# Moving one of four small weight-folding steps from inside a projection stage to the border before the output stage, with a new order of the output parts

## Chip, cores, metric

One core of a Trainium2 chip (trn2). The metric is device time in microseconds (us) of one execution, inputs and outputs in HBM. Lower is better.

## The reference, cut to what matters

Two attention blocks on the same 2048 x 1024 input, mixed by a gate. Block A is linear attention with 32 heads of 32, block B a dilated local attention:

```python
x = A_x
g = _sigmoid((x * gate_w).sum(-1, keepdims=True))
a = _A_ref(x, A_wqkv, A_wo)      # ... num = einsum("bhqd,bhde->bhqe", pq, kv); o = num / den; o @ wo
b = _B_ref(x, B_wqkv, B_wo)      # ... 8 keys per query, two apart; o @ wo
return g * a + (1 - g) * b
```

In block A each head's `kv` is only 32 x 32. The kernel multiplies it into that head's 32 rows of `A_wo` once, which gives a matrix "W2", so that the output is `pq` (normalized) times W2 and no `num` is ever made.

## The kernel before

TensorE works through: A's keys, a Gram matrix, `kv`; a stage with B's values and A's queries (here "value stage"); a B stage, in which B's keys and queries are projected as 64x64 matmuls with the attention in between; and an output stage, 128x128 matmuls that add A's and B's output products in one bank. W2 is made in four "events". Each folds one quarter of it (`g` chooses four of the eight row blocks, `half` the columns): 16 matmuls of 32x32 with 512 columns, one on each 32x32 part of the array, into four PSUM banks, and four copies that write the result over the old weights.

```python
def w2_event(g, half, engines=(nc.vector.tensor_copy, nc.scalar.copy)):
    def go():
        w2p = [ps_1.tile([P, 512], F32, name="w2_ps", tag="p1") for _ in range(4)]
        for j in range(4):
            for r in range(4):
                rs = slice(32 * r, 32 * r + 32)
                nc.tensor.matmul(w2p[r][32 * j:32 * j + 32, :],
                                 lhsT=KVT[rs, 4 * g + j, (r % 2) * 32:(r % 2) * 32 + 32],
                                 rhs=WoA[half][rs, 4 * g + j, :], start=True, stop=True)
        for r in range(4):
            engines[r % len(engines)](out=WoA[half][:, 4 * g + r, :], in_=w2p[r][:])
    return go

units = [u for t in range(4) for u in v_units(t)]        # one 128x128 matmul each
w2_event(0, 0)()
interleave(units, [(20, w2_event(0, 1)), (40, w2_event(1, 0))])
# ... twelve times: 16 value matmuls, 16 query matmuls
w2_event(1, 1, (nc.scalar.copy,))()
# ... B stage, then the output stage:
parts = [(tb, c0, n) for tb in range(NB)                 # row block, first column, columns
         for c0, n in ([(0, 512), (512, 512)] if tb < NB - 1 else [(0, 512), (512, 256), (768, 128), (896, 128)])]
first = [out_part(i, *p_) for i, p_ in enumerate(parts[:7])]
for k in range(2):          # A's half of seven parts, then B's half of them
    for f in first:
        f(k)
# ... then one part after the other; odd parts take banks of ps_3, even ones of ps_pj
```

So the first event lies between the `kv` matmuls (128x64) and the value stage, the second and third lie inside the value stage, the fourth lies between it and the B stage.

The softmax here doesn't subtract the row's maximum and nothing guards it: scores larger than these inputs give would overflow.

Of the kernel before, what the change touches and what calls it, by code (L numbers as in the profile page):

```python
# [11 lines left out]
F32 = mybir.dt.float32  # L12
# [3 lines left out]
P = 128  # L16
# [11 lines left out]
def interleave(units, events):  # L28

    events = sorted(events, key=lambda e: e[0])  # L30
    for i, unit in enumerate(units):
        while events and events[0][0] <= i:
            events.pop(0)[1]()
        unit()
    for _, fn in events:
        fn()
# [3 lines left out]
def kernel(  # L40
# [11 lines left out]
    nc = tc.nc  # L52
# [12 lines left out]
    NB = S // P  # L65
# [10 lines left out]
    def load_w(name, src, col0, tag, only=(0, 1)):  # L76
        halves = []
        for h in only:
            w = wpool.tile([P, KT, 512], BF16, name=f"{name}{h}", tag=tag)
            c0 = col0 + h * 512  # L80
            nc.sync.dma_start(out=w[:], in_=src[:, c0:c0 + 512].rearrange("(kt p) n -> p kt n", p=P))
            halves.append(w)
        return halves
# [19 lines left out]
    with tc.manual_schedule(engines={SP, mybir.EngineType.Activation}):  # L103
# [17 lines left out]
        WoA = load_w("WoA", A_wo, 0, "wo")  # L121
# [18 lines left out]
    for slot in range(2):  # L140
        nc.gpsimd.memset(qsel[:, slot:slot + 1], 0.0)
        for pair in range(2):
            r = 64 * pair + 32 * slot
# [5 lines left out]
    KVT = consts.tile([P, KT, 64], BF16, name="KVT")  # L149
# [3 lines left out]
    def phi(work, dst, pj):  # L153
# [2 lines left out]
        nc.vector.tensor_scalar(out=e[:], in0=e[:], scalar1=1.0, scalar2=1e-6, op0=ALU.min, op1=ALU.add)  # L156
        nc.vector.scalar_tensor_tensor(out=dst, in0=pj[:], scalar=0.0, in1=e[:], op0=ALU.max, op1=ALU.add)

    with tc.manual_schedule(engines={PE}):

        with ExitStack() as s1:
            ps_1 = s1.enter_context(tc.tile_pool(name="ps_1", bufs=4, space=bass.MemoryType.PSUM))
# [41 lines left out]
            for t in range(1, NB):  # L204
                side.append(lambda t=t: nc.vector.tensor_tensor(
                    out=zacc[:], in0=zacc[:] if t > 1 else pk[:, 0, :], in1=pk[:, t, :], op=ALU.add))
            side.append(lambda: nc.gpsimd.partition_all_reduce(zrow[:], zacc[:], P, bass_isa.ReduceOp.add))
            for t in range(NB):
                side.append(lambda t=t: nc.vector.tensor_tensor_reduce(
                    out=gjunk[:], in0=xrow[:, t, :], in1=gw_row[:], scale=1.0, scalar=0.0, op0=ALU.mult,  # L210
# [3 lines left out]
            for half in range(2):  # L214
                g_ = junk.tile([P, KT, 512], BF16, name=f"G{half}", tag=f"G{half}")
                G.append(g_)
                for kt in range(KT):
                    pj = ps_pj.tile([P, 512], F32, name="g_ps", tag="pj")
                    for t in range(NB):
                        nc.tensor.matmul(pj[:], lhsT=xrow[:, t, kt * P:(kt + 1) * P],  # L220
                                         rhs=pk[:, t, half * 512:(half + 1) * 512],
                                         start=(t == 0), stop=(t == NB - 1))
# [11 lines left out]
            for g in range(2):  # L234
                kvp = ps_pj.tile([P, 512], F32, name="kv_ps", tag="pj")[:, 0:256].rearrange("p (c d) -> p c d", c=4)
                for c in range(4):
                    for kt in range(KT):
                        for j in range(2):
                            cols = slice(c * P + 64 * j, c * P + 64 * j + 64)
                            nc.tensor.matmul(kvp[64 * j:64 * j + 64, c, :], lhsT=WvA[g][:, kt, cols],  # L240
                                             rhs=G[g][:, kt, cols], start=(kt == 0), stop=(kt == KT - 1))
# [32 lines left out]



            def w2_event(g, half, engines=(nc.vector.tensor_copy, nc.scalar.copy)):
                def go():
                    w2p = [ps_1.tile([P, 512], F32, name="w2_ps", tag="p1") for _ in range(4)]
                    for j in range(4):  # L280
                        for r in range(4):
                            rs = slice(32 * r, 32 * r + 32)
                            nc.tensor.matmul(w2p[r][32 * j:32 * j + 32, :],  # L283
                                             lhsT=KVT[rs, 4 * g + j, (r % 2) * 32:(r % 2) * 32 + 32],
                                             rhs=WoA[half][rs, 4 * g + j, :], start=True, stop=True)
                    for r in range(4):
                        engines[r % len(engines)](out=WoA[half][:, 4 * g + r, :], in_=w2p[r][:])
                return go

            def v_units(t):  # L290
                def mm(half, kt, st):
                    if kt == 0:
                        st["pj"] = bank1()
                    nc.tensor.matmul(st["pj"][:], lhsT=xT[:, kt, t * P:(t + 1) * P], rhs=WvB[half][:, kt, :],  # L294
                                     start=(kt == 0), stop=(kt == KT - 1))
                    if kt < KT - 1:
                        return
                    v = Vst[t % 2]
                    nc.scalar.copy(out=v[:, half * 16:(half + 1) * 16, 0:Dh],  # L299
                                   in_=st["pj"][:].rearrange("p (h e) -> p h e", h=16))  # L300
                    if half == 1:
                        nc.sync.dma_start(out=vd[t * P:(t + 1) * P, :], in_=v.rearrange("p h e -> p (h e)"))
                        if t % 8 == 7:
                            load_v(t // 8)
                for half in range(2):
                    st = {}
                    for kt in range(KT):
                        yield lambda half=half, kt=kt, st=st: mm(half, kt, st)
# [35 lines left out]
                    nc.sync.dma_start(out=pqd[t * P:(t + 1) * P, :], in_=pn)  # L344

            units = [u for t in range(4) for u in v_units(t)]
            w2_event(0, 0)()
            interleave(units, [(20, w2_event(0, 1)), (40, w2_event(1, 0))])
            for t in range(12):
                for u in v_units(4 + t):  # L350
                    u()
                for u in qa_units(t, bank1, qa_finish):
                    u()
            w2_event(1, 1, (nc.scalar.copy,))()
            WqB = load_w("WqB", B_wqkv, 0, "wc")


# [4 lines left out]
        with ExitStack() as s2:  # L362
# [164 lines left out]
            for c in range(KT):  # L527
                kts[c] = kpool.tile([P, 2, 1024], BF16, name="kt", tag="kt")
                for hh in range(2):
# [3 lines left out]
                    if 1 <= c <= 2:  # L533
                        t = 2 * (c - 1) + hh
                        nc.sync.dma_start_transpose(out=pqT[0][:, :, t * P:(t + 1) * P],
                                                    in_=pqd[t * P:(t + 1) * P, :])
                    if 4 <= c < 7:
# [6 lines left out]
                              in_=B_wo[4 * P:, 512:1024].rearrange("(k p) n -> p k n", p=P))  # L544
# [20 lines left out]
        with ExitStack() as s3:  # L565
            work3 = s3.enter_context(tc.tile_pool(name="work3", bufs=3))
            ps_3 = s3.enter_context(tc.tile_pool(name="ps_3", bufs=4, space=bass.MemoryType.PSUM))
            pqT.append(big.tile([P, KT, 1536], BF16, name="pqT1", tag="vV"))
            for r0 in (512, 1024):
                nc.sync.dma_start_transpose(out=pqT[1][:, :, r0 - 512:r0], in_=pqd[r0:r0 + 512, :])  # L570

            def qa_late(t):
                r = raw[:, t - 12, :]
                for half in range(2):
                    h = slice(half * 512, (half + 1) * 512)
                    phi(work3, r[:, h], r[:, h])
                pn = lw[:, t - 12, :]
                normalize(t, r, pn, fw[:, t % 2, :])
                nc.sync.dma_start_transpose(out=pqT[1][:, :, (t - 4) * P:(t - 3) * P], in_=pn)

            def out_part(i, tb, c0, n):

                st = {}

                def mm(side, c):
                    if side == 0 and c == 0:
                        st["ps"] = ps_3.tile([P, 512], F32, name="e3_ps", tag="p3") if i % 2 else \
                            ps_pj.tile([P, 512], F32, name="d3_ps", tag="pj")
                    if side == 0:
                        lhsT, W = (pqT[0][:, c, tb * P:(tb + 1) * P] if tb < 4 else  # L590
                                   pqT[1][:, c, (tb - 4) * P:(tb - 3) * P]), WoA
                    else:
                        lhsT, W = OBT[:, c, tb * P:(tb + 1) * P], WoB
                    nc.tensor.matmul(st["ps"][:, 0:n], lhsT=lhsT, rhs=W[c0 // 512][:, c, c0 % 512:c0 % 512 + n],  # L594
                                     start=(side == 0 and c == 0), stop=(side == 1 and c == KT - 1))
                    if side == 0 or c < KT - 1:
                        return
                    osb = work3.tile([P, 512], BF16, name="osb", tag="e")
                    dst = rows(out2, tb * P, (tb + 1) * P)[:, c0:c0 + n]
                    if i == len(parts) - 1:  # L600
                        nc.vector.tensor_scalar(out=osb[:, 0:n], in0=st["ps"][:, 0:n], scalar1=omg[:, tb:tb + 1],  # L601
                                                scalar2=None, op0=ALU.mult)
                        nc.sync.dma_start(out=dst, in_=osb[:, 0:n])
                        return
                    nc.scalar.activation(out=osb[:, 0:n], in_=st["ps"][:, 0:n], func=ACT.Copy,
                                         scale=omg[:, tb:tb + 1])
                    nc.scalar.dma_start(out=dst, in_=osb[:, 0:n])

                def side(k):
                    for c in range(KT):  # L610
                        mm(k, c)
                return side

            parts = [(tb, c0, n) for tb in range(NB)
                     for c0, n in ([(0, 512), (512, 512)] if tb < NB - 1 else [(0, 512), (512, 256), (768, 128), (896, 128)])]
            first = [out_part(i, *p_) for i, p_ in enumerate(parts[:7])]
            for k in range(2):
                for f in first:
                    f(k)
            for i, p_ in enumerate(parts):  # L620
                if i < 7:
                    continue
                if i % 2 == 1 and i < 15:
                    qa_late(12 + (i - 7) // 2)
                f = out_part(i, *p_)
                f(0)
                f(1)
# [31 lines left out]
```

## Time and profile before

| | before |
|---|---|
| time, median of three runs | 472.55 us (472.46 to 472.68) |
| span of the profiled run | 471.2 us |
| TensorE busy | 467.1 us |
| value stage, from its first weight load to the B stage's | 98.11 us |
| B stage, from its first weight load to the output stage's | 140.65 us |
| output stage, from its first weight load to the start of the last VectorE instruction | 110.86 us |

From the page of before, busy time of each engine, and the chain that ended last:

```profile
PE 467.1 (99%) x5765; PEld 270.9 (57%) x5765; DVE 276.6 (59%) x600; ACT 168.0 (36%) x274; POOL 15.4 (3%) x30
...
PE 98%; DMA 1%; DVE 0%; issue 0%; DVEq 0%
```

The view of waits of before, for TensorE (who waited for what: us in total, times, longest):

```profile
PE warm L175 <- PEq L643: 0.8, 1, 0.8
PE pk_ps L169 <- DMA xT<-in_A_x_dram: 0.5, 1, 0.5
```

TensorE never waits for another engine after its start. Whatever the change does, it must do it to TensorE's own stream, or by a new wait of TensorE.

The chain of before in order of time (start, length, what), around the first three events. `w_ps` is an event, `p_ps` are value matmuls:

```profile
116.50 2.15 PE kv_ps L240 x128
118.64 0.36 PE w_ps L283 x16
119.01 4.42 PE p_ps L294 x20
123.43 0.36 PE w_ps L283 x16
123.80 4.42 PE p_ps L294 x20
128.22 0.36 PE w_ps L283 x16
```

Read the distance from one row's start to another's, not the lengths: 119.01 to 123.80 is 4.79 us for twenty matmuls and one event, while twenty matmuls alone take 20 x 0.2158 = 4.32 us.

The timeline of before at the edge of B stage and output stage, weight loads only (start, length, line, shape, count, idle time before and what ended it):

```profile
356.23 1.06 PEld L389 LDWEIGHTS <-xT 64*64 64x64 bf16 x20
357.69 0.11 PEld L594 LDWEIGHTS <-pqT 128*128 128x128 bf16 x2 [0.41 <-issue]
```

No event is here, and yet the weight loads pause 0.41 us, for nothing that the profile can name: the array changes from 64x64 to 128x128. The matmuls lose less than this pause. Within a form each weight load starts 0.21 us, one slot, ahead of its matmul; the first one after a change starts together with it (0.004 us ahead here), so only about 0.1 us of the pause is lost time, as measured below.

### The profile page before, as it was taken

Reading aid. Unit: us, or ns where it says so; the run is one execution under the profiler, and the core shown is the slowest. Engines: PE = TensorE matmul, PEld = TensorE weight load, DVE = VectorE, ACT = ScalarE, POOL = GpSimd, SP = SyncE. Lnnn points to the kernel's source line nnn. Section 1 sums busy time; section 2 is a strip of 40 time slices with the busy share of each in tenths; the row PEclk is TensorE's granted clock in tenths of the full one; section 3 lists DMA queues with packets and bytes.
Section 4 is the critical chain, followed back from the end, with each engine's and each line's share of the span. In section 5 each row is a group of like instructions: output and inputs, shape, how many; then the busy total and the mean of one; then the engine's idle time right before and its main releaser. Section 6 shows DMA issues by size and latency. Waiting matters only on the chain.

```text
span 471.2 us, 13192 instructions
## 1 busy us (share of the span) xinstructions
PE 467.1 (99%) x5765; PEld 270.9 (57%) x5765; DVE 276.6 (59%) x600; ACT 168.0 (36%) x274; POOL 15.4 (3%) x30
## 2 busy tenths in 40 slices
PE   8999999999999999999999999999999999999997
PEld 5444444445444444444888888888875444444444
DVE  0596689990319999999667676767660049800000
ACT  1343321102433333334555555555551134221121
POOL 3300000500000000000000000000000000000000
PEclk9999999999999999999999999999999999999999
DMA  8999970000643233527326526432563913221001
GB/s 206 208 234 379 349 255 0 0 1 0 217 137 112 85 142 126 155 97 246 106 57 103 115 50 93 101 87 57 94 168 71 230 61 79 70 54 45 34 33 46
DMA packets 98732, 55.40 MB, mean 118 GB/s; under 512 B 70130, under 2 KB 90610, under 8 KB 98674
## 3 DMA queue, kind: packets, MB, share of 16 engines
q1 hardware_dynamic: 93378, 49.87, 41.1%
q10 hardware_dynamic: 5296, 4.69, 3.0%
q8 instruction: 45, 0.74, 0.7%
q14 instruction: 13, 0.11, 0.1%
HBM read 26.10 MB, written 15.86 MB: 89 GB/s over the span
## 4 chain that ended last, share of the span: by engine, by line
PE 98%; DMA 1%; DVE 0%; issue 0%; DVEq 0%
PE q_ps L389 26%; PE d_ps L594 12%; PE pk_ps L169 12%; PE p_ps L294 12%; PE g_ps L220 12%; PE e_ps L594 12%; PE p_ps L330 9%; PE po L469 2%; PE s2b L447 2%; DMA xT<-in_A_x_dram 1%; PE kv_ps L240 0%; PE w_ps L283 0%; DVE osb L601 0%; DVEq L601 0%
## 5 line engine op out<-in xcount | busy, mean ns | idle before, releaser
L389 PE MATMUL q_ps<-xT,WqB 64*64 64x512 bf16 x1024 | 70.3, 376 | 0.0
L389 PE MATMUL q_ps<-xT,WkB 64*64 64x512 bf16 x1024 | 69.8, 376 | 0.0
L156 DVE TENSOR_SCALAR e<-e 128x512 f32<-128x512 f32 x64 | 27.1, 423 | 66.3 <-ACT e L155 66.3
L294 PE MATMUL p_ps<-WvB,xT 128*128 128x512 bf16 x256 | 57.6, 379 | 0.0
L169 PE MATMUL pk_ps<-WkA,xT 128*128 128x512 bf16 x256 | 55.8, 381 | 0.5 <-DMA xT<-in_A_x_dram 0.5
L220 PE MATMUL g_ps<-pk,xrow 128*128 128x512 bf16 x256 | 55.4, 379 | 0.0
L452 ACT ACTIVATE PT<-s2b 128x928 bf16<-128x928 f32 (+4 forms) x40 | 34.2, 856 | 50.0 <-PE s2b L447 49.0
L454 DVE TENSOR_TENSOR PT<-PT,mask 128x928 bf16<-128x928 bf16 (+4 forms) x40 | 23.6, 590 | 35.6 <-ACT PT L452 35.5
L389 PEld LDWEIGHTS <-WkB 64*64 64x64 bf16 x1024 | 40.3, 107 | 7.0 <-DMA vd<-tmp 0.2
L330 PE MATMUL p_ps<-WqA,xT 128*128 128x512 bf16 x192 | 43.4, 379 | 0.0
L594 PEld LDWEIGHTS <-pqT 128*128 128x128 bf16 x272 | 26.0, 98 | 29.8 <-issue 0.4
L594 PEld LDWEIGHTS <-OBT 128*128 128x128 bf16 x272 | 26.0, 98 | 29.3
L169 PEld LDWEIGHTS <-xT 128*128 128x128 bf16 x256 | 25.0, 98 | 31.0 <-DMA xT<-in_A_x_dram 0.8
L389 PEld LDWEIGHTS <-WqB 64*64 64x64 bf16 x1024 | 39.4, 107 | 5.6 <-DVE qz L429 0.2
L220 PEld LDWEIGHTS <-xrow 128*128 128x128 bf16 x256 | 25.0, 98 | 30.2
L294 PEld LDWEIGHTS <-xT 128*128 128x128 bf16 x256 | 24.8, 98 | 30.2 <-issue 0.7
L601 DVE TENSOR_SCALAR osb<-e_ps,omg 128x128 bf16<-128x128 f32 x1 | 0.4, 351 | 57.6 <-PE e_ps L594 57.6
L155 ACT ACTIVATE e<-pk_ps 128x512 f32<-128x512 f32 x32 | 18.9, 597 | 40.7 <-PE pk_ps L169 36.5
L469 PEld LDWEIGHTS <-PT 64*56 64x56 bf16 (+2 forms) x1152 | 30.1, 104 | 4.4
L330 PEld LDWEIGHTS <-xT 128*128 128x128 bf16 x192 | 18.8, 98 | 22.7
L299 ACT CAST tmp<-p_ps 128x512 bf16<-128x512 f32 x32 | 18.8, 589 | 36.1 <-PE p_ps L294 32.5
L594 PE MATMUL d_ps<-WoA,pqT 128*128 128x512 bf16 (+1 forms) x136 | 30.9, 370 | 0.0
(63 smaller groups left out, 543.5 us busy)
## 6 DMA issues: line engine op xcount, KB each, us to landing
vd<-tmp SPq DMA_DIRECT2D x16, 264.0 KB
xrow<-in_A_x_dram SPq DMA_DIRECT2D x4, 1024.0 KB
out_dram<-osb ACTq DMA_DIRECT2D x31, 128.0 KB
pqd<-tmp SPq DMA_DIRECT2D x12, 256.0 KB
WvA<-in_A_wqkv_dram SPq DMA_DIRECT2D x2, 1024.0 KB
WoA<-in_A_wo_dram SPq DMA_DIRECT2D x2, 1024.0 KB
WvB<-in_B_wqkv_dram SPq DMA_DIRECT2D x2, 1024.0 KB
WqA<-in_A_wqkv_dram SPq DMA_DIRECT2D x2, 1024.0 KB
```

Source lines behind the costliest of these rows:

```text
L155: nc.scalar.activation(out=e[:], in_=pj[:], func=ACT.Exp)
L156: nc.vector.tensor_scalar(out=e[:], in0=e[:], scalar1=1.0, scalar2=1e-6, op0=ALU.min, op1=ALU.add)
L169: nc.tensor.matmul(pj[:], lhsT=xT[:, kt, t * P:(t + 1) * P], rhs=WkA[half][:, kt, :], start=(kt == 0), stop=(kt == KT - 1))
L220: nc.tensor.matmul(pj[:], lhsT=xrow[:, t, kt * P:(kt + 1) * P], rhs=pk[:, t, half * 512:(half + 1) * 512], start=(t == 0), stop=(t == NB - 1))
L294: nc.tensor.matmul(st["pj"][:], lhsT=xT[:, kt, t * P:(t + 1) * P], rhs=WvB[half][:, kt, :], start=(kt == 0), stop=(kt == KT - 1))
L299: nc.scalar.copy(out=v[:, half * 16:(half + 1) * 16, 0:Dh], in_=st["pj"][:].rearrange("p (h e) -> p h e", h=16))
L330: nc.tensor.matmul(st["pj"][:], lhsT=xT[:, kt, t * P:(t + 1) * P], rhs=WqA[half][:, kt, :], start=(kt == 0), stop=(kt == KT - 1))
L389: nc.tensor.matmul(banks[o][64 * j:64 * j + 64, :], lhsT=lhsT(r, kt, j), rhs=rhs(r, kt), start=first and kt == 0, stop=kt == KT - 1, skip_ ...
L452: nc.scalar.activation(out=pt[:, :, 0:W_], in_=s2b[:].rearrange("p a b s -> p (a b) s")[:, :, 0:W_], func=ACT.Exp, scale=SCALE)
L454: nc.vector.tensor_tensor(out=pt[:, :, 0:W_], in0=pt[:, :, 0:W_], in1=mask[:, None, base:base + W_].broadcast_to([P, 4, W_]), op=ALU.mult)
L469: nc.tensor.matmul(o2[64 * h:64 * h + w, par, s_, i, :], lhsT=pt[r, i, o:o + w], rhs=V[r, m, 4 * c + i, :], start=True, stop=True)
L594: nc.tensor.matmul(st["ps"][:, 0:n], lhsT=lhsT, rhs=W[c0 // 512][:, c, c0 % 512:c0 % 512 + n], start=(side == 0 and c == 0), stop=(side == ...
```

## The change

The intent is to take one of the two events out of the value stage, where it interrupts a stream of one form, and put it where the form changes anyway. Three events shift by one place, so that the last of them, (1, 1), falls between B stage and output stage. It rewrites column half 1, so the first four output parts now all take half 0, to give the copies time.

```diff
+    def w2_event(g, half, pool, tag, engines):      # body as before, banks from `pool`; now ahead of all stages
...
-            w2_event(0, 0)()
-            interleave(units, [(20, w2_event(0, 1)), (40, w2_event(1, 0))])
+            both = (nc.vector.tensor_copy, nc.scalar.copy)
+            w2_event(0, 0, ps_1, "p1", both)()
+            interleave(units, [(32, w2_event(0, 1, ps_1, "p1", both))])
...
-            w2_event(1, 1, (nc.scalar.copy,))()
+            w2_event(1, 0, ps_1, "p1", (nc.scalar.copy,))()
...
             ps_3 = s3.enter_context(tc.tile_pool(name="ps_3", bufs=4, space=bass.MemoryType.PSUM))
+            w2_event(1, 1, ps_3, "p3", (nc.scalar.copy,))()
...
-            parts = [(tb, c0, n) for tb in range(NB)
-                     for c0, n in ([(0, 512), (512, 512)] if tb < NB - 1 else [(0, 512), (512, 256), (768, 128), (896, 128)])]
+            parts = [(tb, c0, 512) for t0 in range(0, NB - 1, 4) for c0 in (0, 512) for tb in range(t0, min(t0 + 4, NB - 1))]
+            parts += [(NB - 1, c0, n) for c0, n in ((0, 512), (512, 256), (768, 128), (896, 128))]
```

More of the change, by code (lines that the diff above doesn't have):

```diff
@@ L157, in phi, with go @@
         nc.vector.scalar_tensor_tensor(out=dst, in0=pj[:], scalar=0.0, in1=e[:], op0=ALU.max, op1=ALU.add)
+    def w2_event(g, half, pool, tag, engines):
+        def go():
+            w2p = [pool.tile([P, 512], F32, name="w2_ps", tag=tag) for _ in range(4)]
+            for j in range(4):
+                for r in range(4):
+                    rs = slice(32 * r, 32 * r + 32)
+                    nc.tensor.matmul(w2p[r][32 * j:32 * j + 32, :],
+                                     lhsT=KVT[rs, 4 * g + j, (r % 2) * 32:(r % 2) * 32 + 32],
+                                     rhs=WoA[half][rs, 4 * g + j, :], start=True, stop=True)
+            for r in range(4):
+                engines[r % len(engines)](out=WoA[half][:, 4 * g + r, :], in_=w2p[r][:])
+        return go
     with tc.manual_schedule(engines={PE}):
@@ L273, in bank1 @@
                 return ps_pj.tile([P, 512], F32, name="p1_ps", tag="pj")
-            def w2_event(g, half, engines=(nc.vector.tensor_copy, nc.scalar.copy)):
-                def go():
-                    w2p = [ps_1.tile([P, 512], F32, name="w2_ps", tag="p1") for _ in range(4)]
-                    for j in range(4):
-                        for r in range(4):
-                            rs = slice(32 * r, 32 * r + 32)
-                            nc.tensor.matmul(w2p[r][32 * j:32 * j + 32, :],
-                                             lhsT=KVT[rs, 4 * g + j, (r % 2) * 32:(r % 2) * 32 + 32],
-                                             rhs=WoA[half][rs, 4 * g + j, :], start=True, stop=True)
-                    for r in range(4):
-                        engines[r % len(engines)](out=WoA[half][:, 4 * g + r, :], in_=w2p[r][:])
-                return go
             def v_units(t):
```

## The prediction

> **What bounds the kernel.** TensorE. The page has PE busy 467.1 of 471.2 us at full clock, and the chain that ended last is 98% PE. In the view of waits PE waits 0.8 and 0.5 us at the start, and never again. So only what changes PE's own stream, or makes PE wait, moves the time.
>
> **What one event costs today.** In the chain of waits, 20 value-projection matmuls start at 119.01 us, the event follows, and the next 20 start at 123.80 us; the third event comes another 4.79 us later. Twenty such matmuls need 20 x 0.2158 = 4.32 us (256 took 55.25 us). So an event inside the stage costs 0.47 us. Its 16 32x32 matmuls start within 0.04 us and stream together, one slot of 0.216 us. The other 0.26 us is two changes of array form, 128x128 to 32x32 and back: in the timeline LDWEIGHTS idles 0.42 us before each event and 0.23 us after it, released by "issue". The Trainium skill, "TensorEngine Tiling (Array Packing)", section Tiling Modes, says a change of tiling mode drains the TensorE; these gaps agree.
>
> **What the change does.** Four events stay four; the first, and the one before the B stage, cost as before. Of the two inside the value stage one goes, -0.47 us; the other moves from unit 20 to 32, which is free, since the events at 20 (inside an accumulation) and 40 (between two) cost the same. The one that goes lands between the B stage (64x64) and the output stage (128x128), where a change of form is already paid: the last four 64x64 matmuls start at 357.30 us, the next slot would be 357.52, the first output matmul starts at 357.70, a gap of 0.18 us. With the event this becomes one slot (0.22) and two changes (0.10 to 0.18 in, 0.15 out), so +0.29 to +0.37 us. Net on PE, all on the chain: -0.10 to -0.18 us, about -0.14.
>
> **Why no new wait should appear.** The event needs the banks of the B stage's scores and outputs, last read at 353.5 us. ScalarE first has two evacuations of the last quad (357.80 to 358.87), then four copies, which took 2.05 us at the other edge: bank 0 is free at about 359.4, all at 360.9. The second output part takes bank 0 at about 359.75, a margin of 0.3 us, the tightest point. The new part order delays the first use of the rewritten half of W2 to about 365.8 us, 5 us after the copies; in the old order the second part would have needed it at about 360.6 and stalled some 0.3 us. The row blocks that the new order takes first are in place from the B stage; the later ones keep their index or come later, so the reorder itself costs nothing.
>
> **Prediction.** 472.4 us, 8 in 10 between 472.1 and 472.75. Chances: faster by over 2% 0.003, within 2% 0.992, slower 0.005.
>
> **What the profile would show.** One event fewer in the value stage, and the B stage starting about 0.47 us earlier; between last quad and first output matmul about 0.5 us from slot to slot, with 16 small matmuls in it; the output stage as long as before, without a wait of PE on ScalarE; this event's copies right after the last two evacuations.
>
> **What would make it wrong.** A wait of the second part for the first copy; a dearer change from 64x64 to 32x32; copies scheduled behind other work, stalling output parts; a start of the first loads that varies by more than the effect.

## The result, and the profile after

After took 472.52 us in the median of six runs (472.19 to 473.01), before 472.52 us in six (472.35 to 472.90). The ratio is 0.9999, interval 0.9986 to 1.0012: the same. A ratio here is the mean time of one kernel's fast runs over that of the other's fast runs of the same rounds, so not quite the ratio of the medians quoted. All these runs are at full clock. The interval is 0.13% wide on each side, some 0.6 us. It cannot show an effect of 0.1 us; the traces can.

The chain of after around the two events that are left at this place:

```profile
118.60 0.36 PE w_ps L165 x16
118.96 0.32 PE p_ps L294
...
119.34 6.64 PE p_ps L294 x30
125.98 0.36 PE w_ps L165 x16
126.34 0.75 PE p_ps L294 x3
```

One event is left inside the value stage, after 32 value matmuls. (Some 30 matmul records are missing in this trace, which breaks its rows with short "issue" pieces; the weight loads are all there, so lengths of stages are taken from them.)

The timeline of after at the edge of B stage and output stage, weight loads only:

```profile
356.24 0.35 PEld L390 LDWEIGHTS <-xT 64*64 64x64 bf16 x8
356.99 0.14 PEld L165 LDWEIGHTS <-KVT 32*32 32x32 bf16 x16 [0.41 <-issue]
357.36 0.55 PEld L596 LDWEIGHTS <-pqT 128*128 128x128 bf16 x4 [0.23 <-issue]
```

The pause of 0.41 us now stands ahead of the event. The event adds what follows: 357.36 - 356.99 = 0.37 us.

The timeline of after at the same place, matmuls and ScalarE (rows of other engines left out):

```profile
357.11 1.07 ACT L559 CAST raw<-q_ps 128x512 bf16<-128x512 f32 x2 [0.65 <-PE q_ps L390]
...
358.07 2.07 ACT L169 CAST WoA<-w_ps 128x512 bf16<-128x512 f32 x4
...
359.10 1.89 PE L596 MATMUL e_ps<-WoA,pqT 128*128 128x512 bf16 x8
```

The four copies follow the last two evacuations of the B stage at once and end at 358.07 + 2.07 = 360.14 us. The second output part (`e_ps`) starts at 359.10 us with no wait; the view of waits of after lists only the same two waits at the start (0.8 and 0.4 us).

The lengths of the three stages, from the starts of single weight loads in the traces (in us, same definitions as in the table of before):

| trace | value stage | B stage with the edge | output stage | sum |
|---|---|---|---|---|
| before | 98.106 | 140.648 | 110.860 | 349.614 |
| before, second trace (x11) | 98.107 | 140.462 | 110.861 | 349.430 |
| new order of parts only (x5) | 98.106 | 140.477 | 110.860 | 349.443 |
| after | 97.636 | 140.830 | 110.862 | 349.328 |
| event moved, old order of parts (x6) | 97.637 | 140.831 | 110.861 | 349.329 |

The value stage lost 0.470 us, the edge gained 0.353 to 0.368 us (140.830 less 140.477 or 140.462), the output stage is as it was. Net -0.10 to -0.12 us, or 0.02% of the time. The first trace of before looks 0.29 us slower than after, but 0.17 us of that is a pause in its B stage that x5 and x11, the same instructions there, don't have. That pause is treated under x10 and x11.

### The profile page after: what moved, and what is told of

The parts are those of the page before. It is cut to its first block, busy times and chain, and to the rows that moved or that the text cites. A ratio compares the mean times of both kernels' runs of the same rounds, so it can differ in the third digit from the quotient of the medians.

```text
span 470.9 us, 13162 instructions
## 1 busy us (share of the span) xinstructions
PE 465.3 (99%) x5735; PEld 269.8 (57%) x5765; DVE 275.3 (58%) x598; ACT 169.1 (36%) x276; POOL 15.3 (3%) x30
## 4 chain that ended last, share of the span: by engine, by line
PE 86%; SPq 10%; DMA 2%; issue 1%; DVE 0%; DVEq 0%
PE q_ps L390 26%; PE d_ps L596 12%; PE p_ps L294 12%; PE e_ps L596 11%; PE g_ps L233 11%; PE p_ps L330 9%; SPq L115 4%; SPq L81 3%; DMA WvB<-in_B_wqkv_dram 2%; PE po L470 2%; PE s2b L448 2%; SPq L94 1%; SPq L98 1%; SPq L89 1%; SPq L119 1%
```

## The experiments

All results are correct, except x7's.

Theory: an event costs one matmul slot (0.216 us, 16 small matmuls at once) plus its changes of array form, each about 0.1 us; an event between two stages of different form saves one change, and nothing else in the change matters. Rivals, by the letters of the expectations: the cost is something else (A: a wait for data; B: the small matmuls themselves); the edge is dearer (C) or hides the event wholly (E); the new order of parts itself costs or saves (D); the second output part does not depend on ScalarE at all (F).

### x1 and x2: ten more events, apart and together

After, with the same small matmuls run eleven times instead of once in the value stage, into the same four banks; only the last result is copied. In x1 four value matmuls lie between two runs:

```diff
-interleave(units, [(32, w2_event(0, 1, ps_1, "p1", both))])
+interleave(units, [(20 + 4 * i, early) for i in range(10)] + [(60, last)])   # early: the 16 matmuls alone
```

In x2 all eleven stand back to back at unit 60 (`for _ in range(11)` around the 16 matmuls).

> After, with the 16 small matmuls of the event inside the value stage run ten more times into the same four banks, each time with four value matmuls in between; only the last is copied out, the result stays right. Theory (each event is one slot of 0.216 us and two changes of array form): ten more cost 10 x 0.46 = 4.6 us over after. Rival A (an event costs its small matmuls' starts and little more, the rest being a wait for data that only the real one has): under 1 us.

> After, with the same ten more events of the value stage, but all eleven back to back, so that the array changes form only twice. Theory: 10 x 0.216 = 2.2 us over after, less than half of the separated ones. Rival B (the cost sits in the small matmuls, not in the change of form): 4.6 us, as separated.

x1 took 477.29 us against 472.57 us of before (ratio 1.0101, 1.0084 to 1.0118); x2 took 475.18 us (1.0055, 1.0040 to 1.0070). The chain of x1 in order of time:

```profile
123.27 0.36 PE w_ps L163 x16
123.63 0.97 PE p_ps L298 x4
124.60 0.36 PE w_ps L163 x16
...
127.27 0.36 PE w_ps L163 x16
127.63 0.97 PE p_ps L298 x4
128.60 0.36 PE w_ps L163 x16
```

From event to event it is 1.33 us, four matmuls take 4 x 0.2158 = 0.86 us, so 0.47 us per event, as for the one that the change took out. The timeline of x2, TensorE:

```profile
131.61 2.65 PE L163 MATMUL w_ps<-WoA,KVT 32*32 32x512 bf16 x176
134.41 1.89 PE L298 MATMUL p_ps<-WvB,xT 128*128 128x512 bf16 x8 [0.16 <-issue]
```

All 11 x 16 = 176 small matmuls are one block. (The idle 0.16 us in the second row is a missing matmul record, not a wait.) By the weight loads, the value stage grew against after by 102.347 - 97.636 = 4.711 us in x1 and by 99.847 - 97.636 = 2.211 us in x2: 0.471 us for an event that stands alone, 0.221 us for one that follows another. The 16 matmuls do cost one slot, and the other 0.25 us of a lone event comes with the two changes of form. It can be split by single matmul starts in the trace of before (123.054, then the small ones from 123.364 to 123.414, then 123.730 and 123.957 us): the step in is 0.310 us and the step out 0.316 us, each 0.1 us over a slot; 0.05 us pass while the sixteen start one after the other, and the slot after it is 0.01 us longer than usual. Rivals A and B fall.

### x3: the edge event eleven times

As x2, at the edge: `w2_event(1, 1, ps_3, "p3", (nc.scalar.copy,), times=11)`.

> After, with the event at the edge of B stage and output stage run eleven times back to back. Theory: 2.2 us over after, as in the value stage, and the step from the last 64x64 matmul to the first small one stays at 0.31 us, as does the step out. Rival C (events at this edge are dearer than inside the value stage): clearly more than 2.2 us.

It took 474.86 us (ratio 1.0051, 1.0036 to 1.0066). The timeline of x3 at the edge, weight loads:

```profile
356.85 2.55 PEld L163 LDWEIGHTS <-KVT 32*32 32x32 bf16 x176 [0.41 <-issue]
359.63 0.76 PEld L600 LDWEIGHTS <-pqT 128*128 128x128 bf16 x5 [0.23 <-issue]
```

The B stage with the edge was 143.243 us, 2.413 us over after. Within the block of small loads one step took 0.237 us; it is one of the pauses discussed under x10, some 0.2 us. The rest, 2.2 us, is as in x2. The step from the last 64x64 matmul to the first small one was 0.306 us and the step out 0.308 us. The edge is no dearer place for an event.

### x4: eight events among 64x64 matmuls

After, with eight more runs of the small matmuls, two slots apart, in the last two quads of the B stage:

```diff
-interleave([u for i in range(2) for u in quad_units(late[4 * i:4 * i + 4])], between(512, 576))
+extra = [(48 + 2 * i, lambda: w2_matmuls(1, 1, banks4)) for i in range(8)]   # banks the stage has done with
+interleave([u for i in range(2) for u in quad_units(late[4 * i:4 * i + 4])], between(512, 576) + extra)
```

> After, with eight more runs of the last event's small matmuls put between the 64x64 matmuls of the last two quads, two slots apart, into banks that the B stage has done with; nothing reads them, the result stays right. Theory: a change between 64x64 and 32x32 costs the same as one between 128x128 and 32x32, so 8 x 0.46 = 3.7 us over after. Rival C (64x64 to 32x32 is dearer or cheaper): under 3 or over 4.5 us.

It took 476.28 us (ratio 1.0081, 1.0066 to 1.0096). The timeline of x4, weight loads:

```profile
353.04 0.14 PEld L163 LDWEIGHTS <-KVT 32*32 32x32 bf16 x16 [0.41 <-issue]
353.41 0.14 PEld L394 LDWEIGHTS <-xT 64*64 64x64 bf16 x8 [0.23 <-issue]
353.96 0.14 PEld L163 LDWEIGHTS <-KVT 32*32 32x32 bf16 x16 [0.41 <-issue]
```

The pauses are 0.41 us into the small form and 0.23 us out of it, the same as from 128x128. The B stage grew by 144.737 - 140.830 = 3.907 us, 0.488 us per event; expected were 0.46, and a lone event among 128x128 matmuls takes 0.471. Most of that difference is in the second slot after a change: it came 0.240 us after the first, against 0.227 us among 128x128 matmuls and 0.216 within a form. A change between 64x64 and 32x32 thus costs nearly what one between 128x128 and 32x32 does.

### x5 and x6: the two halves of the change alone

x5 is before with the new order of parts; x6 is after with the old order (the two lines of `parts` exchanged).

> Before, with only the new order of the output parts; all four events stay where they were. Theory: the order is free, the output stage takes the same 110.86 us from its first weight load to the last VectorE instruction, within 0.05 us. Rival D (the new order itself saves or costs, by row blocks or output stores that come at other times): the output stage changes by 0.1 us or more.

> After, with the old order of the output parts, so that the second part uses the rewritten half. Prediction on record: the second part stalls some 0.3 us for the copies. From the trace of after the copies run from 358.07 to 360.14 us, one every 0.5 us, and the second part would need them from 359.96 to 360.61 us in turn, so the first three are in time and the last with 0.4 us to spare: no stall, if each matmul waits only for its own copy; if the first waits for all four, a stall of about 0.2 us.

x5 took 472.59 us (ratio 0.9978, 0.9952 to 1.0004), x6 472.55 us (0.9976, 0.9950 to 1.0003); before had three runs of 474.3 us and more in these rounds, for which see x10. The output stage took 110.860 us in x5 and 110.861 us in x6, against 110.860 us in before: the order of parts is worth nothing by itself, and the event doesn't need it. The timeline of x6:

```profile
358.08 2.08 ACT L169 CAST WoA<-w_ps 128x512 bf16<-128x512 f32 x4
359.12 1.89 PE L596 MATMUL e_ps<-WoA,pqT 128*128 128x512 bf16 x8
...
360.84 1.89 PE L596 MATMUL d_ps<-WoA,pqT 128*128 128x512 bf16 x8
```

In the old order the second part (`e_ps`) uses the rewritten quarter from its fifth matmul on, 359.12 + 4 x 0.216 = 359.98 us. The copies end one by one until 360.16 us, the last matmul of the part that needs one starts at 359.12 + 7 x 0.216 = 360.63 us, and no matmul waits: the third part starts 1.72 us after the second, eight slots. The stall of "some 0.3 us" that the prediction saw in the old order does not exist.

### x7: without the edge event

After without the line that calls it; W2's last quarter stays wrong.

> After, without the event at the edge of B stage and output stage (the result is wrong on purpose). Theory: the step from the last 64x64 matmul to the first output matmul is 0.31 us, against 0.31 + 0.05 + 0.32 us with the event, so 0.36 us less in this place and no other stage changes by more than the hiccups of 0.16 us that the profile of before shows once in the B stage. Rival E (the edge hides the event wholly or for the most part): a difference below 0.2 us.

The timeline of x7 at the edge, weight loads:

```profile
356.13 0.36 PEld L390 LDWEIGHTS <-xT 64*64 64x64 bf16 x7
356.90 2.49 PEld L595 LDWEIGHTS <-pqT 128*128 128x128 bf16 x13 [0.41 <-DMA obd<-Ob]
```

The 0.41 us pause is there without any event (the transfer named was put down to it by this trace; the same pause is put down to "issue" in before). From the last 64x64 matmul to the first output matmul it is 0.308 us, in after 0.306 us to the first small matmul and 0.366 us more to the first output matmul. So the edge does not hide the event: it hides one of its two changes of form. Rival E falls. The B stage of x7 has a pause of its own (140.690 us), so its total says nothing more.

### x8 and x9: copies that come late

After with three useless ScalarE copies of the first bank ahead of the four real ones. In x8 the instruction scheduler put the real ones in between; in x9 ScalarE is held to program order.

```diff
+def slow_copy(out, in_):
+    if not slow:
+        for _ in range(3):
+            nc.scalar.copy(out=dull[:], in_=in_)
+    slow.append(1)
+    nc.scalar.copy(out=out, in_=in_)
-w2_event(1, 1, ps_3, "p3", (nc.scalar.copy,))()
+w2_event(1, 1, ps_3, "p3", (slow_copy,))()     # x9: with ScalarE in program order
```

> After, with three useless ScalarE copies of the first bank ahead of the four copies at the edge, about 1.5 us more on ScalarE. From the trace of after bank 0 is free at 358.66 us and the second output part starts at 359.10 us, a margin of 0.44 us. Theory: the second part now waits 1.5 - 0.44 = about 1.1 us, and the total is about 1.1 us longer. Rival F (the second part doesn't wait for ScalarE here at all): no change.

> As the run with late copies, but with ScalarE held to program order at the edge, so that all three useless copies come before the four real ones (there they were interleaved, and only one came before the copy that frees the bank). In that run one useless copy (0.5 us) made the second output part wait 0.11 us, a margin of 0.39 us in after. Theory: three useless copies take 1.45 us, so the second part waits about 1.05 us and the output stage becomes 110.86 + 1.05 = 111.9 us. Rival F (the second part doesn't depend on ScalarE): 110.86 us.

x8 took 472.68 us (ratio 0.9993, 0.9954 to 1.0031), not the 1.1 us more that was expected: only one useless copy came before the first real one, and the output stage was 110.966 us, 0.11 us longer. x9 took 474.10 us (1.0021, 1.0003 to 1.0040), with an output stage of 112.155 us, 1.29 us longer. The view of waits of x9, its first line:

```profile
PE e_ps L610 <- ACT WoA L580: 1.1, 1, 1.1
```

And its timeline:

```profile
358.73 1.84 ACT L578 COPY dull<-w_ps 128x512 f32<-128x512 f32 x3
...
360.47 2.06 ACT L580 CAST WoA<-w_ps 128x512 bf16<-128x512 f32 x4
361.11 1.89 PE L610 MATMUL e_ps<-WoA,pqT 128*128 128x512 bf16 x8 [1.13 <-ACT WoA L580]
```

The real copies began 360.47 - 358.73 = 1.74 us after the useless ones, and the part was 1.29 us late: some 0.4 us of slack is used up first. So the second part does wait for ScalarE when ScalarE is late, and in after it has about 0.4 us to spare. Rival F falls; the amount was underestimated because the useless copies, all into one tile, came 1.74 / 3 = 0.58 us apart, not 0.48 as in x8.

### x10 and x11: both kernels once more

Unchanged, for a second trace of each and five more rounds of after.

> After, unchanged, once more in five rounds with before. Theory: value stage 97.636 us, output stage 110.86 us as in every run so far, B stage 140.83 us, or up to 0.5 us more if a late instruction block falls into it; the total 0.1 us less than before in the mean, which the spread of single runs (0.3 us and more) will not resolve. Rival D (the change is worth some tenths that one profile missed): an interval that excludes 1.

> Before, unchanged, for a second profile. Theory: value stage 98.106, output stage 110.86 us as before; if the 0.17 us in the B stage was chance (x5, the same program up to the output stage, has 140.477 us there), the B stage is 140.48 us or differs from 140.648 us; if it belongs to the program, it is 140.648 us again.

x10 took 472.44 us in the median of six runs (472.20 to 474.52), ratio 0.9999 (0.9981 to 1.0016). Value and output stage repeat to 0.001 us in both. The B stage does not: x11 has 140.462 us where before had 140.648, and x10 has 140.938 us where after had 140.830. The timeline of before shows the pause, weight loads:

```profile
350.37 0.34 PEld L389 LDWEIGHTS <-xT 64*64 64x64 bf16 x6
350.98 0.36 PEld L389 LDWEIGHTS <-xT 64*64 64x64 bf16 x11 [0.27 <-issue]
```

Seven of the thirteen traces have one or two such pauses late in the B stage, of 0.11 us (x10) to 0.77 us (x2, two). By number in TensorE's stream they all fall on weight load 5087, 5215 or 5343, which are 128 apart, though the kernels do different work there. 128 pairs of load and matmul are 256 instructions. The page of before, its part on DMA queues (packets, MB, share of time), has

```profile
q8 instruction: 45, 0.74, 0.7%
```

for the whole run: 45 packets of 0.74 MB / 45 = 16 KB, and 45 x 256 = 11,520 is close to TensorE's 2 x 5765 = 11,530 instructions; x1 to x4, with 256 to 320 more, have 46 packets. The Trainium skill, "Runtime: NRT & Kernel Launch", section Instruction fetch mechanics, says that an engine's instructions are fetched in blocks of 16 KiB, 256 instructions, and that crossing a boundary is "mostly hidden". A late block fits the places, and the times of the packets in the traces speak for it. At each of the eight pauses the weight load before it had started only 0.57 to 1.23 us after the latest packet of q8 landed; in the nine traces in which load 5087 does not pause it was 1.30 us or more. Of the four that pause there, the later the packet, the longer the step to load 5087: 0.73 us in x9 (the load before it started 0.57 us after the landing), 0.41 in x7 (1.09), 0.38 in before (1.12), 0.28 in x10 (1.23). Against it, six loads at such places in 128x128 stages came as soon (0.82 to 1.19 us) without a pause; and no run tested it by moving transfers away. So the cause is likely, but argued, not shown. What is shown is that the pauses come and go between traces of one program.

The run of 474.52 us in x10 has another cause, and its trace shows it. The timeline of x10 at the start of the keys' matmuls, weight loads, two of eight such rows:

```profile
6.06 0.15 PEld L182 LDWEIGHTS <-xT 128*128 128x128 bf16 x1 [0.28 <-issue]
...
9.05 0.15 PEld L182 LDWEIGHTS <-xT 128*128 128x128 bf16 x1 [0.28 <-issue]
```

In before there is one such row, and the next one already holds 22 loads:

```profile
6.26 4.64 PEld L169 LDWEIGHTS <-xT 128*128 128x128 bf16 x22 [0.28 <-issue]
```

In x10 they come every 0.43 us, twice the slot of 0.216: the first matmuls run at half clock. Full clock is granted from 9.54 us in this trace and from 6.26 us in before, and x10's value stage starts at 120.68 us instead of 118.94. The Trainium skill, "TensorE: Matmul & The Clock Gate", Part 1, says that the clock is raised by a window that runs freely and not from the kernel's start; these two traces agree: their first matmuls, useless ones to warm up, start at 0.84 us in both, and yet full clock comes 3.3 us apart. The other runs of 474 us of before and x8 may be the same; they have no trace.

No experiment gave a version faster than both kernels. An event behind another costs 0.22 us instead of 0.47, but a second event at the same edge would need four more PSUM banks, which by the code the matmuls that follow take at once. Two events back to back at this or an earlier border were not tried.

## Why the prediction was right, and where it was off

- **TensorE bounds the kernel, only its own stream counts.** Right. Stage lengths account for the difference.
- **An event inside the stage costs 0.47 us, one slot and two changes of form.** Right: 0.470 us came out of the value stage, x1 gives 0.471 per event, x2 separates 0.221 for the slot from 0.25 that comes with the two changes. (The sixteen matmuls start within 0.05 us, not 0.04 as the prediction read; nothing hangs on it.) The Trainium skill, "TensorEngine Tiling (Array Packing)", Tiling Modes, says that a change of mode drains the TensorE. The traces agree and add the size: the step between the last matmul start of one form and the first of the next is 0.305 to 0.318 us at every event and edge of all thirteen traces (from the value stage on, and where no matmul record is missing), against 0.216 within a form, so some 0.1 us each. What the 0.1 us consists of is not separated: that the first weight load of the new form does not start ahead of its matmul would fit an array that must empty first, but also an unhidden load (one takes 0.09 to 0.1 us), and no run tells the two apart.
- **"a gap of 0.18 us" paid already at the edge.** Mis-sized. The prediction took 357.30 us as the start of the last four 64x64 matmuls; that is the start of the first of them. In this trace the four start one after the other over 0.086 us (in x5 and x11, which have no pause before, over 0.025 us), and the last one starts at 357.389 us and the first output matmul at 357.697, a step of 0.308 us, so the change paid already is 0.308 - 0.216 = 0.09 us. The added event thus costs 0.35 to 0.37 us, the upper end of "+0.29 to +0.37 us", and the net is -0.10 to -0.12 us instead of "about -0.14". The rule behind it held: moving an event to an edge saves one change of form.
- **No new wait, a margin of 0.3 us for the second part.** Right; the margin is 0.4 us (x9), and the wait is real when ScalarE is later than that.
- **"in the old order the second part ... stalled some 0.3 us".** Wrong. x6 has no stall. The prediction's times, copies until 360.9 us and the fifth matmul at 360.6, are times of the trace of before, where the edge lies 0.7 us later than in after (the last evacuations start at 357.80 us there and at 357.11 in after); so 360.1 instead of 360.9 is mostly that shift. Two things were misjudged: ScalarE starts the copies 0.11 us before the last evacuation ends, which shortens the stall from 0.3 to about 0.2 us; and, what removes the rest, the part needs the four pieces one after the other over 0.65 us, not all at its fifth matmul.
- **The reorder costs nothing.** Right (x5), and by x6 it buys nothing today either; it keeps the edge safe from ScalarE being late, no more.
- **The total.** 472.52 us lies in the range 472.1 to 472.75 and "same" had 0.992. The effect that the traces show, 0.1 us, is about a sixth of the interval's half width; two comparisons gave 0.9999. So the total would have come out as predicted for any effect this small: it says nothing for the mechanism, which only the stage lengths and x1 to x7 test.

## What to carry to other kernels

On TensorE, count changes of array form as well as matmuls: here each costs about 0.1 us, an interruption has two (with the staggered start of its matmuls 0.25 us over its own slot), and moving it to a place where the form changes anyway saves exactly one, while putting two interruptions together saves both of one, 0.25 us. For effects below the spread of runs compare stages between fixed weight loads in the traces; they repeat to 0.002 us, but check a second trace of the same program before you believe a difference in one stage. Before adding a protective reorder, ask when each single operand is first used and when it is ready.

## What the Trainium skill lacked or had wrong

- "TensorEngine Tiling (Array Packing)" says that a change of mode drains the array but gives no cost. Here the step across a change was 0.305 to 0.318 us against 0.216 us within a form, for 128x128 to 32x32, 64x64 to 32x32, 64x64 to 128x128 and 32x32 to both.
- The same page and "TensorE: Matmul & The Clock Gate", Part 3, treat one packed group at a time. A train of eleven groups of 16 small matmuls with 512 columns, each with its weights loaded anew, cost 0.221 us per further group (x2): the weight loads were hidden.
- "Runtime: NRT & Kernel Launch", Instruction fetch mechanics, calls the cost of a block boundary "mostly hidden". Pauses of 0.1 to 0.6 us at single places 256 TensorE instructions apart appeared in seven of thirteen traces; the landing times of the instruction packets fit late blocks as their cause, which no run tested.
